# y's step issued in two pieces with other products between them, one convolution moved from TensorE to VectorE, and the loads of later chunks tied to products

## The chip, the cores and the metric

The kernel runs on one core of a Trainium2 chip. The metric is the device time of one execution, in microseconds (us). TensorE is called PE here, its weight loads PEld, VectorE DVE, ScalarE ACT, GpSimd POOL, and the engine that issues the transfers SP. TensorE's clock has two levels, 1.2 and 2.4 GHz; the profile gives the granted clock of a stretch as a share of the higher one.

## The reference

A gated linear attention feeds a gated projection with a short causal convolution. There are 4 batches, 8 heads, 768 steps and a head size of 48; the projection is 384 wide, and the convolution has 5 taps.

```python
# attention, for every batch and head
f = 1.0 / (1.0 + np.exp(-f_logit))
for t in range(S):
    state = f[:, :, t, :, None] * state + np.einsum('bhd,bhe->bhde', k[:, :, t], v[:, :, t])
    y[:, :, t] = np.einsum('bhd,bhde->bhe', q[:, :, t], state)
# projection of x = y with the heads side by side
for k in range(K):
    gate_pre += conv_w[k][None, None, :] * xp[:, k:k + S, :]
gate = 1.0 / (1.0 + np.exp(-gate_pre))
return gate * (x @ w_val) @ w_out
```

## The kernel before

The 768 steps are cut into six chunks (c = 0 to 5) of 128. A tile holds two heads of a pair side by side on the partitions, so four batches of four pairs make 16 blocks of 128 columns. Batches are called b, and h = 0 or 1 is a half, that is two batches.

For a chunk, `loadf`, `loadk`, `loadq` and `loadv` bring the inputs (SP). `pexp`, `pln`, `scan`, `exp2` and `exp1` make the decays (ACT and DVE). `pmulk` and `pmulq` scale k and q by them (DVE). On PE, `ktrans` transposes k, `scores` makes the products of q and k inside the chunk, `dstate` the products of k and v for the state, and `apply` makes y: from the masked scores with v (matmuls that the profile names psum<-asb,vb) and, from chunk 1 on, from q with the state (psum<-qb,st). `mask` (DVE, asb<-psum,tri) puts the scores into SBUF, `kevac` (ACT, ksb<-psum) the transposes, and `xevac` (ACT, xf<-psum) puts y there. `stadd` (DVE, u<-st,psum) and `stmul` (POOL, st<-u,e) carry the state on.

The projection of a chunk follows. `msplit` and `mlow` split y into a high and a low part; `mval` is x @ w_val in nine matmuls; `mout` is the product with w_out, nine more. The convolution has two forms. `pconv` does it on PE, in 120 small matmuls against diagonal matrices (psum<-xf,diag), and `gate` reads its PSUM. `mlast` (ACT) and twelve `mconv` (DVE, gt<-xf,cws,gt) do the same without PE. Chunks 0, 1 and 2 use `pconv`, chunks 3, 4 and 5 `mlast` and `mconv`. The last chunk's projection goes in two halves, numbered 5 and 6. `weight` is one step of the conversion of the 64-bit weights to pairs of float32, spread over POOL, ACT and DVE; `wload` loads them, and `wturn` moves a second copy of w_out within SBUF, for the chunks without `pconv`.

The order of all this work is written out in the string PROGRAM, one word a piece, and every engine does its pieces in exactly that order: the class Ordered ties each instruction of an engine to the one before it. So a piece that has to wait holds up all that stands behind it on its engine. SP's queue, which issues all transfers, is ordered in the same way. PSUM has eight banks, which pieces take and give back in the order of the string.

`apply` for a half h issues two passes, n = 0 and n = 1. Row half r of the array (partitions 0 to 63, or 64 to 127) works on batch 2h + (r ^ n), so that the two row halves never write the same PSUM bank at once. Between the passes stands `PE.drain()`, after which the second pass adds to what the first has written. From chunk 1 on a pass is 96 matmuls, in chunk 0 it is 64. Each matmul is two instructions, a weight load and the product.

Of the kernel before, what the change touches and what calls it, by code (L numbers as in the profile page):

```python
# [37 lines left out]
pmulq 0 0; ktrans 0 3; halo 0; weight 1; kevac 0 0; loadv 0 0; weight 0; scores 0 3; loadv 0 1; weight 0; mask 0 2;
pmulk 0 1; exp1 0 1; pmulq 0 1; weight 1; mask 0 3; ktrans 0 1; pexp 1 0; loadv 0 2; ktrans 0 2; pln 1 0; kevac 0 1;
exp1 1 1; weight 1; scores 0 0; dstate 0 0; scan 1 0; kevac 0 2; mask 0 0; weight 1; weight 0; loadk 1 0; weight 3;  # L40
weight 2; dstate 0 1; exp2 1 0; exp1 1 0; weight 3; scores 0 1; apply 0 1; mask 0 1; dstate 0 2; okc 0; pmulk 1 0;
apply 0 0; weight 2; loadq 1 0; pmulq 1 0; kevac 0 3; loadv 1 0; xevac 0 1; ktrans 1 0; dstate 0 3; kevac 1 0;
weight 2; ktrans 1 1; weight 0; scores 1 1; loadk 1 1; xevac 0 0; weight 2; weight 3; pconv 0; mask 1 1; weight 2;
stadd 0 0; msplit 0; loadf 2 0; weight 2; kevac 1 1; stadd 0 1; pexp 2 0; weight 2; weight 3; scores 1 0; weight 2;
pln 2 0; pmulk 1 1; dstate 1 0; mask 1 0; dstate 1 1; gate 0 2; loadq 1 1; weight 1; weight 3; ktrans 1 2; weight 3;
loadv 1 1; loadf 2 1; apply 1 0; weight 2; loadk 2 0; weight 3; ktrans 1 3; kevac 1 2; wload 2; loadf 3 0; weight 3;
weight 3; loadq 2 1; weight 2; stadd 1 0; pmulq 1 1; weight 5; mlow 0; dstate 1 2; halo 1; scan 2 0; scores 1 2;
gate 0 0; xevac 1 0; scores 1 3; weight 3; gate 0 1; mval 0 0; mval 0 2; mask 1 3; okc 1; weight 4; mask 1 2;
pexp 2 1; pln 2 1; mmul 0 0; loadq 2 0; kevac 1 3; scan 2 1; apply 1 1; exp2 2 0; stmul 1 0; pmulk 2 0; pexp 3 0;
weight 4; weight 4; exp1 2 0; loadv 3 0; loadk 2 1; loadv 2 0; dstate 1 3; mval 0 1; mmul 0 2; weight 5; ktrans 2 1;  # L50
xevac 1 1; pmulq 2 0; exp2 2 1; weight 4; ktrans 2 0; weight 5; scores 2 1; kevac 2 1; stadd 1 1; loadf 3 1; weight 4;
weight 4; kevac 2 0; pmulk 2 1; scores 2 0; mask 2 1; weight 5; exp1 2 1; mhigh 0 2; msplit 1; okc 2; stmul 1 1;
pconv 1; loadq 3 0; weight 4; ktrans 2 2; dstate 2 0; pexp 3 1; weight 4; dstate 2 1; pln 3 1; weight 6; mask 2 0;
kevac 2 2; weight 6; loadf 4 0; mmul 0 1; pln 3 0; apply 2 0; pexp 4 0; loadk 4 0; mlow 1; ktrans 2 3; weight 6;
xevac 2 0; mval 1 2; kevac 2 3; pmulq 2 1; loadv 2 1; stadd 2 0; weight 6; stmul 2 0; mhigh 0 1; scan 3 0; scores 2 3;
mask 2 3; loadq 3 1; weight 5; mval 1 0; loadk 3 0; exp2 3 0; scores 2 2; pln 4 0; loadq 4 0; weight 5; weight 5;
loadf 4 1; weight 6; mhigh 0 0; weight 6; wturn 2; exp1 3 0; mask 2 2; weight 6; mrest 0 0; mrest 0 1; mrest 0 2;
gate 1 0; halo 2; gate 1 2; gate 1 1; scan 3 1; mval 1 1; weight 5; weight 6; apply 2 1; mout 0 0; pmulk 3 0;
ktrans 3 0; exp2 3 1; mmul 1 2; pmulq 3 0; loadf 5 0; dstate 2 2; mout 0 1; dstate 2 3; mstore 0 0; loadk 3 1;
wturn 1; kevac 3 0; ktrans 3 1; xevac 2 1; wturn 0; mout 0 2; pmulk 3 1; loadv 4 0; pexp 4 1; pexp 5 0; mmul 1 0;  # L60
scores 3 0; msplit 2; loadq 4 1; mmul 1 1; kevac 3 1; dstate 3 0; mhigh 1 2; dstate 3 1; mhigh 1 0; stadd 2 1;
pln 4 1; loadv 3 1; scan 4 0; scores 3 1; mask 3 0; loadk 4 1; send 0 0; pln 5 0; stadd 3 0; exp1 3 1; mstore 0 1;
mask 3 1; loadk 5 0; exp2 4 0; mrest 1 0; mstore 0 2; mlow 2; exp1 4 0; scan 4 1; pconv 2; pmulk 4 0; mhigh 1 1;
mrest 1 2; mval 2 2; exp2 4 1; apply 3 0; mrest 1 1; mout 1 0; exp1 4 1; gate 2 1; send 0 1; loadv 4 1; send 0 2;
stmul 2 1; gate 2 0; mstore 1 0; mout 1 1; scan 5 0; pmulq 3 1; loadf 5 1; pmulq 4 0; wturn 3; pmulq 4 1; halo 3;
mval 2 1; xevac 3 0; pmulk 4 1; stmul 3 0; gate 2 2; pexp 5 1; mmul 2 2; scores 3 2; scores 4 1; scores 3 3; exp2 5 0;
mmul 2 1; pln 5 1; mval 2 0; mask 4 1; mout 1 2; mask 3 3; mstore 1 1; ktrans 3 2; send 1 0; scan 5 1; exp1 5 0;
mask 3 2; mmul 2 0; loadq 5 0; pmulk 5 0; mhigh 2 1; mstore 1 2; scores 4 0; mask 4 0; kevac 3 2; mhigh 2 0; send 1 1;
ktrans 3 3; mrest 2 0; apply 3 1; mhigh 2 2; mrest 2 1; scores 4 2; mrest 2 2; kevac 3 3; xevac 3 1; dstate 3 2;
scores 4 3; mlast 3 0; ktrans 4 0; pmulq 5 0; mask 4 2; wturn 4; mconv 3 0 0; mconv 3 0 1; kevac 4 0; dstate 3 3;  # L70
mask 4 3; apply 4 0; mlast 3 1; okc 4; stadd 3 1; mlast 3 2; stmul 3 1; mconv 3 2 0; msplit 3; mconv 3 1 0; mout 2 0;
mout 2 2; exp2 5 1; loadq 5 1; mconv 3 0 2; mconv 3 1 1; apply 4 1; mlow 3; mstore 2 0; dstate 4 0; ktrans 4 1;
loadv 5 0; xevac 4 0; send 2 0; loadk 5 1; mconv 3 2 1; mconv 3 0 3; mstore 2 2; mconv 3 1 2; exp1 5 1; mval 3 1;
scores 5 0; xevac 4 1; halo 4; mconv 3 1 3; kevac 4 1; mout 2 1; okc 5; scores 5 1; dstate 4 1; pmulq 5 1; gate 3 0;
send 1 2; pmulk 5 1; gate 3 1; mmul 3 1; mstore 2 1; mhigh 3 1; mconv 3 2 2; mask 5 1; mconv 3 2 3; wturn 5; halo 5;
ktrans 4 2; gate 3 2; mrest 3 1; mlast 4 1; stadd 4 0; mval 3 2; mval 3 0; ktrans 4 3; mmul 3 2; stmul 4 0; kevac 4 2;
scores 5 2; dstate 4 2; mhigh 3 2; loadv 5 1; mconv 4 1 0; mask 5 0; mconv 4 1 1; kevac 4 3; send 2 2; scores 5 3;
dstate 4 3; mmul 3 0; send 2 1; msplit 4; mrest 3 2; mhigh 3 0; mlow 4; mlast 4 2; mrest 3 0; mconv 4 2 0; apply 5 0;
mask 5 2; mlast 4 0; xevac 5 0; stadd 4 1; mconv 4 2 1; mlast 5 2; mlast 5 0; mconv 4 2 2; mconv 4 1 2; mask 5 3;
mconv 5 0 0; mout 3 0; mout 3 1; mval 4 0; mconv 4 0 0; mstore 3 0; mval 4 2; msplit 5; hint 3; stmul 4 1; okc 3;  # L80
mstore 3 1; mconv 4 0 1; mconv 5 2 0; mconv 4 2 3; mlast 5 1; mconv 5 2 1; apply 5 1; mval 4 1; gate 4 2; mconv 4 1 3;
mout 3 2; mmul 4 2; gate 4 1; mconv 5 0 1; mconv 4 0 2; xevac 5 1; mconv 5 0 2; msplit 6; mconv 5 1 0; mlast 6 2;
mconv 6 2 0; mlow 6; mlast 6 1; mconv 5 0 3; mconv 4 0 3; mlow 5; send 3 0; mval 6 0; mlast 6 0; gate 4 0;
mconv 6 2 1; mhigh 4 2; mval 6 2; mmul 4 1; mhigh 4 1; mval 5 1; mconv 5 2 2; mmul 4 0; mhigh 4 0; mval 5 0; gate 5 0;
mconv 5 1 1; mrest 4 1; mrest 4 2; mconv 5 2 3; mval 6 1; mrest 4 0; mconv 6 2 2; mconv 5 1 2; mconv 5 1 3; mval 5 2;
mconv 6 1 0; mstore 3 2; mconv 6 2 3; gate 5 1; mmul 5 0; gate 5 2; mconv 6 0 0; mhigh 5 0; mmul 5 1; mconv 6 0 1;
mout 4 0; mout 4 1; mmul 5 2; mhigh 5 1; mconv 6 1 1; send 3 1; mconv 6 0 2; gate 6 2; send 3 2; mhigh 5 2;
# [700 lines left out]
```

## Time and profile before

| what | us |
|---|---|
| median of three timed runs | 256.76 (254.6 to 258.27) |
| the profiled execution | 256.75 |
| its span, first to last instruction | 255.0 |
| PE busy, share of the span | 189.5, 74% |
| DVE busy | 163.2, 64% |
| ACT busy | 129.6, 51% |
| POOL busy | 40.9, 16% |
| mean granted clock of PE | 0.928 |

A line of a timeline gives the start, how long the group took, the engine, the operation with the tile that it writes and those that it reads, and the count; what stands in brackets is the idle time of the engine just before it and what ended it. "issue" means that the engine waited for nothing that the profile shows. Nearly all instructions have one line number, that of the helper which orders them, so tiles tell them apart.

### The profile page before, as it was taken

How to read it: one execution, taken by the hardware profiler on the slowest of the kernel's cores; microseconds unless marked ns; L12 is line 12 of the kernel's file. 1: busy time of each engine (PE TensorE's matmuls, PEld its weight loads, DVE VectorE, ACT ScalarE, POOL GpSimd, SP SyncE). 2: the span in 40 equal slices, each digit the busy share in tenths (PEclk: the TensorE clock that was granted, in tenths of full speed). 3: DMA queues.
4: the chain of work that ended last, by engine and by line, in shares of the span. 5: the costliest groups of instructions: out<-in, count | busy, mean ns of one | idle time of the engine just before them, and what ended most of it. 6: DMA issues, size and time to landing. Idle time of an engine off the chain costs nothing. (4 is left out here: it accounts for less than half of the span.)

```text
span 255.0 us, 8960 instructions
## 1 busy us (share of the span) xinstructions
PE 189.5 (74%) x4084; PEld 150.3 (59%) x4084; DVE 163.2 (64%) x228; ACT 129.6 (51%) x203; POOL 40.9 (16%) x47
## 2 busy tenths in 40 slices
...
GB/s 179 394 414 417 389 107 6 226 35 361 112 27 282 17 167 37 312 263 3 136 218 7 124 57 18 157 5 204 109 44 1 5 42 44 3 0 41 59 164 39
DMA packets 11917, 33.30 MB, mean 131 GB/s; under 512 B 1504, under 2 KB 3296, under 8 KB 11616
## 3 DMA queue, kind: packets, MB, share of 16 engines
...
q8 instruction: 34, 0.56, 0.9%
...
## 5 line engine op out<-in xcount | busy, mean ns | idle before, releaser
L106 ACT ACTIVATE e<-e 128x1024 f32<-128x1024 f32 (+2 forms) x58 | 52.4, 930 | 11.2 <-DVE e L106 7.9
L106 DVE TENSOR_TENSOR asb<-psum,tri 128x768 f32<-128x768 f32 x24 | 22.7, 950 | 40.0 <-PE psum L106 28.8
L106 PE MATMUL psum<-asb,vb 64*32 64x64 f32 (+1 forms) x1536 | 29.4, 264 | 16.2 <-issue 15.7
L106 PE MATMUL psum<-rg,woH 128*128 128x512 f32 (+1 forms) x108 | 34.4, 406 | 3.0 <-ACT xf L106 1.9
L106 PEld LDWEIGHTS psum<-asb,vb 64*32 64x32 f32 x1536 | 25.3, 113 | 19.1 <-issue 18.4
L106 ACT COPY xf<-psum 128x768 f32<-128x768 f32 x12 | 9.6, 800 | 42.6 <-PE psum L106 40.0
L106 DVE TENSOR_TENSOR_SCAN e<-keep,e 128x1024 f32<-128x1024 bf16 (+1 forms) x13 | 28.7, 2218 | 4.0 <-ACT e L106 4.0
L106 POOL TENSOR_TENSOR st<-u,e 128x512 f32<-128x512 f32 x8 | 15.4, 1931 | 95.2 <-DVE u L106 81.8
L106 PE MATMUL psum<-ident,kb 128*128 128x128 f32 x80 | 15.5, 331 | 19.2 <-DVE kb L106 16.2
L106 PEld LDWEIGHTS psum<-rg,woH 128*128 128x128 f32 x108 | 20.5, 202 | 7.7 <-ACT xf L106 2.1
L106 PE MATMUL psum<-qb,kb 64*64 64x128 f32 (+1 forms) x768 | 22.2, 259 | 3.4 <-ACT xf L106 2.3
L106 PEld LDWEIGHTS psum<-qb,kb 64*64 64x64 f32 x768 | 19.2, 140 | 8.7 <-ACT xf L106 3.1
L106 PEld LDWEIGHTS psum<-ident,kb 128*128 128x128 f32 x80 | 10.9, 166 | 22.0 <-issue 16.4
L106 ACT COPY osb<-psum 128x512 f32<-128x512 f32 x15 | 8.7, 586 | 26.1 <-PE psum L106 23.5
L106 ACT COPY ksb<-psum 128x384 f32<-128x384 f32 x20 | 9.4, 475 | 23.8 <-PE psum L106 23.8
L106 PE MATMUL psum<-rg,woL 128*128 128x512 f32 (+1 forms) x54 | 21.5, 398 | 0.0
L106 PE MATMUL psum<-xf,diag 32*32 32x512 f32 x360 | 17.4, 652 | 4.7 <-DVE asb L106 4.6
L106 PE MATMUL psum<-xH,wvH 128*128 128x512 f32 x45 | 19.3, 429 | 0.3 <-ACT xf L106 0.3
L106 DVE TENSOR_TENSOR gt<-psum,gt 128x512 f32<-128x512 f32 x15 | 10.1, 685 | 14.5 <-PE psum L106 9.1
L106 DVE SCALAR_TENSOR_TENSOR gt<-xf,cws,gt 128x512 f32<-128x512 f32 x24 | 18.9, 807 | 0.1
L106 PE MATMUL psum<-xL,wvH 128*128 128x512 f32 x45 | 18.2, 405 | 0.0
L106 PE MATMUL psum<-xH,wvL 128*128 128x512 f32 x45 | 18.1, 403 | 0.0
...
## 6 DMA issues: line engine op xcount, KB each, us to landing
e<-in_f SPq DMA_DIRECT2D x11, 512.0 KB, 5.1
kb<-in_k SPq DMA_DIRECT2D x11, 512.0 KB, 5.9
qb<-in_q SPq DMA_DIRECT2D x11, 512.0 KB, 7.2
...
```

The source lines that it names most:

```text
L106: ins = emit(*a, **kw)
```

## The change

- `apply` takes a third number, n, and issues one pass. The drain is gone. A new piece `turn c h` stands in the order between the two passes of a half: a POOL memset of eight numbers (the tile `mark`) that waits for the last PE instruction issued so far, and the first matmul of the second pass waits for that memset. Other PE pieces stand between the passes.
- `load` for chunks 2 and later also waits for the last PE instruction that stands before it in the order.
- The convolution of chunk 2 goes from `pconv` to three `mlast` and twelve `mconv`. So chunk 2's projection uses the second copy of w_out, and the `wturn` pieces come earlier.
- `dstate` makes 48 columns a head and not 64. The state tile st has 80 columns a pair of heads, data in the middle and zeros (one POOL memset at the start) around it; `stadd` and `stmul` handle 48 columns of each.
- The whole order is written anew, under a rule that counts the blocks in which PE's instructions are loaded.

The core of the diff; of the new order, the start, a stretch with chunk 2's convolution, and one line of chunk 5:

```diff
-CONV = "PPPVVV"
+CONV = "PPVVVV"
...
+loadf 0 1; pexp 0 1; pln 0 1; loadf 0 2; loadv 0 1; loadv 0 0; loadf 0 0; loadq 0 1; pexp 0 2; scan 0 1; pln 0 2;
+scan 0 2; loadq 0 0; exp2 0 1; pexp 0 0; loadk 0 2; pln 0 0; loadk 0 0; scan 0 0; loadk 0 1; pmulk 0 1; loadf 1 0;
+wload 0; exp1 0 1; exp2 0 2; pmulq 0 1; loadq 0 2; loadf 2 0; ktrans 0 1; exp2 0 0; pexp 1 0; loadv 0 2; pmulk 0 2;
...
+kevac 0 2; weight 1; pexp 2 0; pmulk 1 0; apply 0 1 0; ktrans 0 3; stadd 0 0; kevac 0 3; apply 0 0 0; weight 2;
+turn 0 0; weight 0; weight 2; weight 1; dstate 0 2; dstate 0 3; loadq 1 0; ktrans 1 1; pmulq 1 0; loadk 1 1; pexp 1 1;
+loadv 1 0; loadv 1 1; ktrans 1 0; kevac 1 0; pln 1 1; turn 0 1; weight 1; kevac 1 1; weight 1; apply 0 0 1; loadq 1 1;
+weight 1; scores 1 0; apply 0 1 1; stadd 0 1; loadk 2 0; weight 1; weight 0; xevac 0 0; xevac 0 1; pln 2 0;
...
+scores 3 3; kevac 3 1; okc 2; mrest 1 2; mrest 1 1; mlast 2 1; loadf 5 0; wturn 5; mconv 2 0 0; wturn 2; mask 3 3;
+apply 3 0 0; turn 3 0; mconv 2 1 0; exp2 4 0; mout 1 0; mask 3 2; dstate 3 0; mlast 2 2; send 0 1; loadq 4 1;
+stmul 2 1; mout 1 1; ktrans 3 2; mconv 2 0 1; exp1 4 0; wturn 4; pexp 5 0; exp2 4 1; mconv 2 1 1; wturn 1;
+mconv 2 2 0; mlow 2; mconv 2 1 2; mconv 2 0 2; dstate 3 1; mconv 2 1 3; kevac 3 2; apply 3 0 1; loadk 4 0; mstore 1 1;
...
+mval 3 2; mask 5 3; apply 5 0 0; mmul 3 2; mhigh 3 2; mrest 3 1; scores 5 2; mrest 3 0; turn 5 0; loadv 5 1; msplit 4;
...
-    st = mp.tile([128, BP, 64], F32, name="st")
+    st = mp.tile([128, BP, 80], F32, name="st")
+    mark = mp.tile([1, 8], F32, name="mark")
-    U = [mp.tile([128, 2 * NP, 64], F32, name=f"u{i}") for i in range(2)]
+    U = [mp.tile([128, 2 * NP, D], F32, name=f"u{i}") for i in range(2)]
...
+    def after(ins, what):
+        tc.add_manual_dep(ins.ins, what.ins.name, mybir.DependencyInfo(mybir.DependencyClass.Sync, mybir.DependencyReason.DATA),
+                          reason="not before that")
     def load(dst, src, c, n):
         x0, x1 = spans["f"](c)[n]
-        SP.dma_start(dst[:, x0:x1], src[c, :, x0:x1])
+        ins = SP.dma_start(dst[:, x0:x1], src[c, :, x0:x1])
+        if c > 1 and PE.last is not None:
+            after(ins, PE.last)
...
+    POOL.memset(st, 0.0)
...
-                us.append((st[rows, x, 32 * (g - r) : 32 * (g - r) + 32], qb[i][rows, x], m, slice(0, C)))
+                us.append((st[rows, x, 16 + 32 * g - 48 * r : 48 + 32 * g - 48 * r], qb[i][rows, x], m, slice(0, C)))
...
-    def apply(c, h):
+    def apply(c, h, n):
+        if n == 0:
+            banks.take(("apply", c, h), 2)
...
-            if n:
-                PE.drain()
...
+            if (c, h) in fence:
+                after(ins, fence.pop((c, h)))
+
+    def turn(c, h):
+        ins = POOL.memset(mark, 0.0)
+        after(ins, PE.last)
+        fence[c, h] = ins
...
-                PE.matmul(dps[s * 64 : s * 64 + 64, n * 64 : n * 64 + 64], KSB[b % 2][:, p, s],
-                          vb[c % NB][:, b * NP + p, 48 * s : 48 * s + 64], start=True, stop=True)
+                PE.matmul(dps[s * 64 : s * 64 + 64, n * D : n * D + D], KSB[b % 2][:, p, s],
+                          vb[c % NB][:, b * NP + p, 64 * s : 64 * s + D], start=True, stop=True)
...
-            DVE.tensor_tensor(out=U[h][:], in0=st[:, HS[h]], in1=dps, op=ALU.add)
+            DVE.tensor_tensor(out=U[h][:], in0=S, in1=dps, op=ALU.add)
```

On PE alone, the new order of the first chunk and a half is: ktrans 0 1; scores 0 1; ktrans 0 0; scores 0 2; scores 0 3; ktrans 0 2; dstate 0 0; dstate 0 1; scores 0 0; apply 0 1 0; ktrans 0 3; apply 0 0 0; dstate 0 2; dstate 0 3; ktrans 1 1; ktrans 1 0; apply 0 0 1; scores 1 0; apply 0 1 1; dstate 1 0; scores 1 1; pconv 0. Its end, from the last half's first pass, is: apply 5 1 0; mval 4 1; mval 4 0; apply 5 1 1; mval 4 2; mout 3 2; mval 5 1; mval 5 2; mval 5 0; mval 6 1; mval 6 2; mval 6 0; and then the mout of 4, 5 and 6. Before, the end was: apply 5 1; mval 4 1; mout 3 2; mval 6 0; mval 6 2; mval 5 1; and on.

## Rows read from the trace of the kernel before

**Rows 1.** The page's first part: busy time of an engine, its share of the span, and its instructions.
```profile
PE 189.5 (74%) x4084; PEld 150.3 (59%) x4084; DVE 163.2 (64%) x228; ACT 129.6 (51%) x203; POOL 40.9 (16%) x47
```
**Rows 2.** Who waited for whom, PE's matmuls alone: us in total, times, the longest in us.
```profile
PE psum L106 <- issue: 18.1, 12, 5.2
PE psum L106 <- DVE kb L106: 16.2, 1, 16.2
PE psum L106 <- DVE asb L106: 12.8, 9, 3.0
PE psum L106 <- ACT xf L106: 4.6, 5, 1.9
```
**Rows 3.** The timeline of PE around stalls that "issue" ended, in both of chunk 0's `apply` and in the first of chunk 1's.
```profile
28.45 1.56 PE L106 MATMUL psum<-asb,vb 64*32 64x64 f32 x83 [0.70 <-issue]
29.94 0.69 PE L106 MATMUL psum<-vb,ksb 128*64 128x64 f32 x16
30.55 0.66 PE L106 MATMUL psum<-asb,vb 64*32 64x128 f32 x28
36.44 2.75 PE L106 MATMUL psum<-asb,vb 64*32 64x128 f32 x100 [5.23 <-issue]
...
52.37 1.00 PE L106 MATMUL psum<-asb,vb 64*32 64x128 f32 x59 [1.43 <-issue]
...
55.70 0.44 PE L106 MATMUL psum<-asb,vb 64*32 64x64 f32 x27 [1.07 <-issue]
```
**Rows 4.** The page's third part, the queue that brings instructions: packets, MB, share of 16 engines.
```profile
q8 instruction: 34, 0.56, 0.9%
```
**Rows 5.** The timeline of PE: one `scores`, the first matmul of an `mval` and the product behind its ninth, two passes of an `apply`, and chunk 2's `pconv` with the product behind it.
```profile
47.59 0.90 PE L106 MATMUL psum<-qb,kb 64*64 64x128 f32 x32
...
95.96 0.51 PE L106 MATMUL psum<-xH,wvH 128*128 128x512 f32 x1
...
98.25 0.90 PE L106 MATMUL psum<-qb,kb 64*64 64x128 f32 x32
...
101.36 0.67 PE L106 MATMUL psum<-qb,st 64*32 64x128 f32 x32
...
102.93 0.67 PE L106 MATMUL psum<-qb,st 64*32 64x128 f32 x32
...
123.90 1.06 PE L106 MATMUL psum<-xf,diag 32*32 32x512 f32 x8 [1.16 <-DVE asb L106]
125.36 4.74 PE L106 MATMUL psum<-xf,diag 32*32 32x512 f32 x112 [0.40 <-DVE asb L106]
130.03 0.50 PE L106 MATMUL psum<-xH,wvH 128*128 128x512 f32 x1
```
**Rows 6.** Busy time by stretch: its length, then PE, PEld, DVE, ACT and POOL busy (instructions), PE's granted clock, the share of the DMA engines, GB/s.
```profile
30.00:45.00 15.00, 9.58 (x266) 7.34 (x277) 4.92 (x9) 4.46 (x7) 0.00 (x0) 0.77 0.25 95
...
105.00:115.00 10.00, 8.68 (x71) 6.70 (x71) 5.83 (x9) 2.86 (x4) 0.00 (x0) 0.66 0.82 290
...
225.00:235.00 10.00, 8.79 (x52) 8.79 (x53) 9.96 (x20) 4.47 (x10) 0.00 (x0) 0.66 0.07 26
```
**Rows 7.** The same view with other stretches: the start, the saturated stretch behind it, the middle, and five us of the middle.
```profile
0.00:16.00 16.00, 0.00 (x0) 0.00 (x0) 10.68 (x12) 11.01 (x17) 5.99 (x20) 1.00 0.87 313
16.00:36.00 20.00, 13.09 (x348) 10.87 (x349) 16.63 (x28) 12.07 (x21) 2.29 (x3) 0.95 0.90 355
...
85.00:165.00 80.00, 65.55 (x1470) 50.42 (x1468) 55.73 (x61) 45.01 (x65) 14.24 (x7) 0.94 0.37 120
...
130.00:135.00 5.00, 4.92 (x191) 4.05 (x188) 5.00 (x6) 4.30 (x5) 0.28 (x1) 1.00 0.44 139
```
**Rows 8.** Groups of instructions with shapes kept apart: count, busy us, mean ns of one, idle before.
```profile
L106 DVE SCALAR_TENSOR_TENSOR gt<-xf,cws,gt 128x512 f32<-128x512 f32 x24 | 18.9, 807 | 0.1
...
L106 DVE TENSOR_TENSOR u<-st,psum 128x512 f32<-128x512 f32 x8 | 5.5, 682 | 8.3 <-ACT xf L106 8.3
...
L106 ACT ACTIVATE gt<-xf,cws 128x512 f32<-128x512 f32 x6 | 4.2, 722 | 1.6 <-DVE rg L106 1.5
...
L106 POOL MEMSET ones<- 128x1 f32 x1 | 0.1, 93 | 0.0
```
**Rows 9.** The start, in the timelines of DVE (two rows) and of PE (one).
```profile
8.73 5.87 DVE L106 TENSOR_TENSOR_SCAN e<-keep,e 128x1024 f32<-128x1024 bf16 x3 [2.50 <-ACT e L106]
14.53 1.93 DVE L106 TENSOR_TENSOR kb<-kb,e 128x512 f32<-128x512 f32 x4
...
16.23 1.19 PE L106 MATMUL psum<-ident,kb 128*128 128x128 f32 x4 [16.23 <-DVE kb L106]
```
**Rows 10.** The timeline of PE's weight loads at the second pass of an `apply`, and that of POOL at the longest of its products.
```profile
67.58 0.41 PEld L106 LDWEIGHTS psum<-qb,st 64*32 64x32 f32 x32 [0.24 <-issue]
...
134.72 5.16 POOL L106 TENSOR_TENSOR st<-u,e 128x512 f32<-128x512 f32 x1 [13.43 <-PE psum L106]
```
**Rows 11.** Transfers by line: count, KB each, median us from issue to landing.
```profile
kb<-in_k SPq DMA_DIRECT2D x11, 512.0 KB, 5.9
qb<-in_q SPq DMA_DIRECT2D x11, 512.0 KB, 7.2
```
**Rows 12.** The timeline of PE where the last half's y has to reach the projection.
```profile
224.41 0.39 PE L106 MATMUL psum<-re,wvH 128*128 128x256 f32 x1 [1.75 <-ACT re L106]
226.21 0.58 PE L106 MATMUL psum<-re,wvH 128*128 128x256 f32 x1 [1.41 <-DVE re L106]
```

More of the change, by code (lines that the diff above doesn't have):

```diff
@@ L38 @@
[L38 to L87, printed above, removed]
@@ new lines @@
+scan 0 2; loadq 0 0; exp2 0 1; pexp 0 0; loadk 0 2; pln 0 0; loadk 0 0; scan 0 0; loadk 0 1; pmulk 0 1; loadf 1 0;
+wload 0; exp1 0 1; exp2 0 2; pmulq 0 1; loadq 0 2; loadf 2 0; ktrans 0 1; exp2 0 0; pexp 1 0; loadv 0 2; pmulk 0 2;
+exp1 0 2; pmulk 0 0; scores 0 1; pmulq 0 2; ktrans 0 0; halo 0; pln 1 0; scan 1 0; scores 0 2; loadk 1 0; weight 0;
+weight 0; kevac 0 0; exp1 0 0; weight 0; pmulq 0 0; weight 0; scores 0 3; wload 1; ktrans 0 2; kevac 0 1; mask 0 2;
+weight 1; dstate 0 0; dstate 0 1; exp2 1 0; exp1 1 0; loadf 1 1; mask 0 3; weight 0; mask 0 1; scores 0 0; mask 0 0;
@@ new lines @@
+weight 2; exp1 1 1; mask 1 0; pconv 0; mask 1 1; weight 3; weight 3; pmulk 1 1; pmulq 1 1; weight 3; apply 1 0 0;
+ktrans 1 3; gate 0 2; turn 1 0; weight 2; dstate 1 1; weight 3; weight 3; weight 3; scores 1 3; gate 0 0; weight 2;
+okc 1; ktrans 1 2; apply 1 0 1; wload 2; weight 4; okc 0; loadf 3 1; kevac 1 3; weight 3; weight 3; stadd 1 0; mlow 0;
+loadv 2 0; scores 1 2; gate 0 1; mval 0 0; weight 4; mask 1 3; weight 2; pexp 2 1; weight 3; mask 1 2; weight 5;
+kevac 1 2; weight 4; apply 1 1 0; weight 3; stmul 1 0; weight 1; weight 1; turn 1 1; loadv 2 1; loadq 2 0; dstate 1 2;
@@ new lines @@
+weight 4; weight 5; mval 0 2; dstate 1 3; pln 2 1; scan 2 0; weight 4; weight 4; loadf 4 0; exp2 2 0; scan 2 1;
+weight 4; halo 1; exp1 2 0; pmulk 2 0; weight 4; apply 1 1 1; loadv 3 0; loadq 2 1; mval 0 1; pexp 3 1; xevac 1 0;
+stadd 1 1; xevac 1 1; weight 6; weight 6; msplit 1; mmul 0 0; mmul 0 2; weight 6; ktrans 2 0; weight 5; mmul 0 1;
+ktrans 2 1; wturn 0; pexp 4 0; loadf 3 0; exp2 2 1; weight 5; kevac 2 0; stmul 1 1; loadf 4 1; kevac 2 1; loadk 2 1;
+exp1 2 1; mhigh 0 2; pln 3 1; weight 6; mhigh 0 1; weight 5; weight 6; pmulq 2 0; loadq 3 0; mlow 1; weight 6;
@@ new lines @@
+pconv 1; scores 2 1; weight 6; mhigh 0 0; mask 2 1; pexp 3 0; loadk 3 0; weight 6; pln 3 0; loadq 3 1; scores 2 0;
+dstate 2 0; weight 5; pmulk 2 1; pexp 4 1; mask 2 0; halo 2; dstate 2 1; weight 5; mrest 0 0; weight 5; pln 4 1;
+mval 1 2; ktrans 2 2; stadd 2 0; apply 2 0 0; mrest 0 2; gate 1 0; mrest 0 1; kevac 2 2; mval 1 0; loadv 3 1;
+scan 3 0; scan 3 1; loadk 3 1; turn 2 0; mmul 1 0; apply 2 0 1; mval 1 1; pmulq 2 1; dstate 2 2; gate 1 2; gate 1 1;
+pln 4 0; xevac 2 0; mout 0 1; exp2 3 0; scan 4 1; scores 2 3; scores 2 2; mstore 0 1; pmulk 3 0; mmul 1 2; mask 2 3;
@@ new lines @@
+mask 2 2; exp2 3 1; mmul 1 1; exp1 3 0; loadv 4 0; loadq 4 0; pmulq 3 0; mout 0 0; scan 4 0; ktrans 2 3; ktrans 3 0;
+apply 2 1 0; mout 0 2; pmulk 3 1; ktrans 3 1; mstore 0 0; send 0 0; kevac 2 3; exp1 3 1; turn 2 1; stmul 2 0;
+scores 3 0; mhigh 1 0; mstore 0 2; apply 2 1 1; kevac 3 0; scores 3 1; mrest 1 0; mask 3 0; pmulq 3 1; send 0 2;
+mhigh 1 1; dstate 2 3; xevac 2 1; mhigh 1 2; mask 3 1; ktrans 3 3; msplit 2; stadd 2 1; mlast 2 0; scores 3 2;
+scores 3 3; kevac 3 1; okc 2; mrest 1 2; mrest 1 1; mlast 2 1; loadf 5 0; wturn 5; mconv 2 0 0; wturn 2; mask 3 3;
@@ new lines @@
+gate 2 2; pln 5 0; xevac 3 0; stmul 3 0; pexp 5 1; mmul 2 2; apply 3 1 1; mout 1 2; scores 4 1; okc 3; pln 5 1;
+pmulq 4 1; wturn 3; pmulk 4 1; mmul 2 0; mhigh 2 2; mval 2 1; scan 5 0; mstore 1 2; xevac 3 1; mhigh 2 0; mask 4 1;
+mrest 2 2; mmul 2 1; scores 4 0; scores 4 2; halo 3; scores 4 3; loadk 5 0; loadq 5 1; dstate 3 3; mask 4 0; mask 4 2;
+exp2 5 0; ktrans 4 0; mhigh 2 1; mrest 2 0; msplit 3; ktrans 4 1; kevac 4 0; ktrans 4 2; apply 4 0 0; stadd 3 1;
+mrest 2 1; dstate 4 0; loadk 5 1; kevac 4 1; mlast 3 1; turn 4 0; scan 5 1; mlast 3 0; send 1 2; mlow 3; mconv 3 0 0;
@@ new lines @@
+loadq 5 0; dstate 4 1; exp1 5 0; kevac 4 2; mconv 3 0 1; mask 4 3; mout 2 1; exp2 5 1; mconv 3 0 2; apply 4 0 1;
+mconv 3 0 3; mconv 3 1 0; mout 2 0; stmul 3 1; ktrans 4 3; mlast 3 2; mconv 3 1 1; kevac 4 3; pmulk 5 0; exp1 5 1;
+send 1 1; pmulk 5 1; mstore 2 1; apply 4 1 0; loadv 5 0; mval 3 1; gate 3 0; send 2 1; mstore 2 0; mconv 3 1 2;
+dstate 4 2; mconv 3 1 3; dstate 4 3; mconv 3 2 0; mconv 3 2 1; pmulq 5 0; xevac 4 0; stadd 4 0; turn 4 1; pmulq 5 1;
+apply 4 1 1; send 2 0; xevac 4 1; stmul 4 0; halo 4; mconv 3 2 2; mout 2 2; gate 3 1; mmul 3 1; mstore 2 2; mval 3 0;
```

63 lines of the change are left out of this document (36 added, 27 removed).

## The prediction

> **What bounds the kernel now.** I read the page's first part to see which engine is fullest, then PE's waits to see where the rest of its time is, then its timeline at the largest waits, and the busy time by stretch for its clock and for what the others have to spare. PE is the fullest, with 189.5 us of the span's 255.0; DVE has 163.2 [rows 1]. The first matmul starts at 16.2 us [rows 9], and after PE's last, at 247.6, some 7.4 us of stores and closing work follow. Between these PE has about 231.4 us, so some 42 us of it are idle. "Issue" ends 18.1 us of that, DVE's masks 12.8 and ACT's copies of y 4.6 [rows 2], and the wait for the last half's y 3.2 [rows 12]. The reader is to see that the largest of these is no data at all.
>
> The "issue" stalls stand inside `apply`, and at even distances: from the one at 28.45 us to the one at 36.44 there are 83 + 16 + 28 = 127 matmuls [rows 3], with their weight loads 254 instructions. The instruction queue moved 0.56 MB in 34 packets, 16.5 KB each [rows 4]. Were a packet 254 instructions, one would be 65 bytes, and PE's 2 x 4084 [rows 1] would make 0.53 MB, nearly all that the queue moved. So PE stops where it has run through a block before the next has come. From 28.45 to 36.44 the next one took 8.0 us, with the DMA engines 90% busy [rows 3, 7]; from 52.37 to 55.70 it took 3.3 [rows 3]. An `apply` of both passes is 192 matmuls, and one pass takes 102.93 - 101.36 = 1.57 us [rows 5], so a block of 127 inside it lasts 2.1 us. That is too short to hide 3.3.
>
> There is a second loss. After idle time PE runs at the lower clock level for part of a stretch: the mean is 0.77 from 30 to 45 us and 0.66 from 105 to 115 (both behind long "issue" stalls), and 0.66 from 225 to 235 [rows 6]. Busy time times the missing share gives 9.58 x 0.23 = 2.2, 8.68 x 0.34 = 3.0 and 8.79 x 0.34 = 3.0 us, worked out from these rows.
>
> **The change part by part.** The sum starts at the profiled execution's 256.75 us, 0.01 below the median of 256.76, so nothing is lost between them.
>
> *Blocks and the two pieces.* I counted the matmuls of both orders in steps of 127 and added up PE's work in each step, a piece at the time from its start to that of the next, such as 1.57 us for a pass or 98.25 - 95.96 = 2.3 for an `mval` [rows 5]. Before, 11 blocks hold less than 2.5 us of work; after, 4 do, since an `mval` or `mout` stands between most passes. The four are at chunk 0's second passes, before chunk 3's first, where apply 3 0 1 and 3 1 0 are adjacent, and around chunk 5's scores 5 2. The two stalls of chunk 0 made 5.9 us [rows 3]; the other ten share 12.2, some 1.2 each. After: 4 x 1.2 = 4.9, and 2.5 more for the start, where the DMA engines stay saturated [rows 7] but chunk 0's blocks get 3.7 and 4.3 us of work. That is 7.4 instead of 18.1, -10.7; the bounds are 0 and -18.1.
>
> The Trainium skill ("Runtime: NRT & Kernel Launch", section "Instruction fetch mechanics") says that instructions come in 16 KiB blocks of 256, the next fetched while the current one runs, and that the cost of a block's end is mostly hidden. The trace agrees on the block, with 254 instructions and 16.5 KB, and not on the hiding, with 18.1 us. By that rule this term would be nothing and the sum 10.7 higher; that is a rival below.
>
> *The drain.* It goes from twelve places. The second pass's weight load stands 0.24 us behind the first pass's [rows 10]; part of that any switch of tiles would cost. I take -2 in all, bounds 0 and -2.9.
>
> *The token.* The memset has a neighbour of 93 ns [rows 8]. With the two hand-overs it is a few tenths. The shortest cover is one `scores`, 0.90 us [rows 5], so I cost it at nothing where POOL is free. If POOL is not, the second pass waits: behind `turn 1 1` stand five weight steps and `stmul 1 0`, and one product on POOL took 5.16 us [rows 10]. I take +1; bounds 0 and +5.
>
> *The convolution of chunk 2.* PE loses the `pconv` from 123.90 to 130.03, 5.7 us without its waits of 1.6 [rows 5]: -5.7. DVE gains 12 x 0.79 = 9.5 us (18.9 / 24) and ACT 3 x 0.72 = 2.2 [rows 8]. DVE has 80 - 55.7 = 24.3 us to spare from 85 to 165, but none in stretches such as 130 to 135 [rows 7]. What hides the twelve is that spare time; where it is gone, masks and `pmulk` come late and PE waits as it did for 12.8 us. The bounds are 0 and +11.7; I take about half, +5.5.
>
> *Narrower state.* A `stadd` of 512 columns takes 682 ns [rows 8]; a quarter less of each of eight gives DVE 1.4 us at most, an estimate; `dstate` issues as many matmuls as before. The memset of st at the start runs while POOL has 10 us to spare [rows 7]. I take -0.5, bounds 0 and -2.
>
> *The start.* Before, DVE did three scans (5.87 us from 8.73) and two `pmulk` before the first `ktrans` [rows 9]; one scan was chunk 1's. The new order leaves that one out and asks for one `pmulk`, of quarter 1. With two scans, about 3.6 us, and 0.8 for the product it comes to 13.2. The loads ahead of it are 3.0 MB; at the start's mean 313 GB/s [rows 7] that is 9.6 us, before which it is hidden, and I add half a microsecond. -2.5, bounds 0 and -3.
>
> *The clock.* With the long stalls gone I take half of the first two stretches' 5.2 us: -2.6, bounds 0 and -5.2.
>
> *The end.* Behind the last pass stood an `mval` and a `mout` before the first product that needs the last half's y; now there are three half-width `mval` more, each half of a 2.3 us product. They cover the 3.2 us of [rows 12]; I take -2.7, and nothing for the clock there. Bounds 0 and -6.
>
> *The later loads.* Each now waits for a product that the order puts well before its use; the shortest distance I find is `loadk 2 1`, issued behind ktrans 2 1 and used after pconv 1 and the pass of scores behind it, some 6 us on, against 5.9 to landing [rows 11]. SP's queue behind a waiting load holds other loads, `wturn` and stores. I take 0, bounds -2 and +26 (below).
>
> Sum: -10.7 - 2 + 1 - 5.7 + 5.5 - 0.5 - 2.5 - 2.6 - 2.7 = -20.2, which is 236.5; I say 236.
>
> **The rivals.** *DVE becomes the bound.* All of the 9.5 and the 2.2 us end up in PE's waits: 6.2 more, and the token's bound with it: about 244. For it: the full stretches [rows 7]. Against it: the spare 24.3 us.
>
> *Instructions come late all the same.* The stalls keep their 18.1 us, at other places, since fetches are slow under loads: 236.5 + 10.7, about 247. For it: the 8.0 us fetch [rows 3]. Against it: 3.3 us where DMA was calmer, and the loads are now spread. The skill's rule named above leads to the same number, for another reason, that the stalls never were fetches.
>
> *Both of these*, 236.5 + 10.7 + 6.2 = 253.4, no change.
>
> *Loads late behind products: slower.* In each of chunks 2 to 5 PE waits for one load of q or k of 5.9 to 7.2 us [rows 11] that was issued as it was needed: 4 x 6.55 = 26.2 gives 263. It decides from about 20 us on, three such waits. For it: one queue in strict order, and most of these loads were issued early before. Against it: the distances above.
>
> *The waits shrink too.* If the 12.8 us for masks [rows 2] fall by 8, as more work stands between a mask and its pass, and the twelve `mconv` find spare time, it is 225.
>
> **How the numbers follow.** The forecast has 0.44, DVE as the bound 0.17, late instructions 0.15, both 0.10, late loads 0.07, shrinking waits 0.07. The forecast's own range is 230 to 242. The range of 226 to 250 takes in the first three and part of the last, and leaves out about 0.2. A change of less than 2%, 5.1 us, can't be told from none here: faster is under 251.6, slower over 261.9. The first three and the last make 0.83, less some spill of the upper ones: 0.80. No change has the case of both and that spill, less what of late loads is slower: 0.13. Slower: 0.07.
>
> **What the profile of the changed kernel would show.** If the blocks are right, "issue" ends 5 to 9 us of PE's waits and hardly any stands at a second pass. If the start is right, the first matmul is at 13 to 14 us. PE's busy time should be near 180, and DVE's near 171. If the token is late, PE waits for POOL's `mark`, first at apply 1 1 1. If DVE binds, the waits for masks grow beyond 15 us between 90 and 130 us. If loads are late, PE or DVE wait for kb or qb behind a DMA. The forecast is wrong above all if the "issue" row stays over 14 us, or if the masks take what it gives back.

## The result

The changed kernel takes 223.79 us (median of 4 runs, 222.83 to 225.06) against 255.68 for the kernel before in the same job. The ratio is 0.8833, 95% interval 0.8723 to 0.8943: about 12% faster. That is 12 us under the forecast of 236 us and 2.2 under the low end of its range, 226 to 250. A ratio here and below compares only the faster runs of a kernel, those within 1.5% of its fastest, so it is not the quotient of the medians. The profiled execution took 224.42 us, 32.3 less than before's.

The page's first part for the kernel after, in answer to [rows 1]:

```profile
span 222.6 us, 8753 instructions
PE 177.0 (80%) x3964; PEld 143.3 (64%) x3964; DVE 168.7 (76%) x240; ACT 130.3 (59%) x206; POOL 32.7 (15%) x60
```

Who PE's matmuls waited for in the kernel after, in answer to [rows 2] (us in total, times, the longest):

```profile
PE psum L110 <- DVE asb L110: 16.7, 12, 5.3
PE psum L110 <- DVE kb L110: 13.3, 2, 13.1
PE psum L110 <- issue: 6.5, 5, 2.2
PE psum L110 <- DVE qb L110: 0.9, 2, 0.4
PE psum L110 <- POOL mark L110: 0.8, 3, 0.3
PE psum L110 <- POOL st L110: 0.5, 1, 0.5
PE psum L110 <- ACT xf L110: 0.5, 2, 0.2
```

With the busy times these make an account of the span as PE sees it:

| PE's time, us | before | after | difference |
|---|---|---|---|
| ahead of the first matmul | 16.2 | 13.1 | -3.1 |
| busy | 189.5 | 177.0 | -12.5 |
| "issue" | 18.1 | 6.5 | -11.6 |
| masks (asb) | 12.8 | 16.7 | +3.9 |
| y into SBUF (xf) | 4.6 | 0.5 | -4.1 |
| the last half's y (re) | 3.2 | none | -3.2 |
| others of those shown | 2.3 | 2.2 | -0.1 |
| behind the last matmul | 7.4 | 6.5 | -0.9 |

The reader is to see three things. The waits on instructions fell as the prediction had it. PE's busy time fell by twice the work that was taken from it. And the waits for masks grew by about as much as those for y into SBUF fell, a row for which the prediction's sum has no term.

The timeline of PE in the kernel after, around what is left of "issue", in answer to [rows 3]:

```profile
13.07 1.19 PE L110 MATMUL psum<-ident,kb 128*128 128x128 f32 x4 [13.07 <-DVE kb L110]
...
24.36 0.35 PE L110 MATMUL psum<-asb,vb 64*32 64x64 f32 x16 [0.64 <-issue]
...
30.29 1.02 PE L110 MATMUL psum<-asb,vb 64*32 64x128 f32 x60 [1.59 <-issue]
...
33.85 0.45 PE L110 MATMUL psum<-asb,vb 64*32 64x64 f32 x29 [1.06 <-issue]
...
44.17 0.74 PE L110 MATMUL psum<-asb,vb 64*32 64x128 f32 x38 [2.22 <-issue]
...
122.11 1.02 PE L110 MATMUL psum<-asb,vb 64*32 64x128 f32 x61 [0.99 <-issue]
```

From 50 us on a single one is left, where the passes 3 0 1 and 3 1 0 are adjacent; the other four lie in chunk 0 and at the first pass of chunk 1. The last of these four, at 44.17, stands behind 127 matmuls with 4.5 us of work, more than half of a `pconv` among them; while they ran, the DMA engines were busy for 0.77 of the time. The first row answers to [rows 9]: PE starts at 13.07.

PE's groups with shapes kept apart (count, busy us, mean ns) show where busy time went:

```profile
L110 PE MATMUL psum<-xf,diag 32*32 32x512 f32 x240 | 9.9, 592 | 0.5 <-POOL st L110 0.5
L110 PE MATMUL psum<-re,wvH 128*128 128x256 f32 x36 | 6.2, 276 | 0.0
L110 PE MATMUL psum<-re,wvL 128*128 128x256 f32 x18 | 5.0, 276 | 0.0
```

Before, the same view has 17.4 us at 652 ns for `pconv` and 9.2 and 6.2 us, at 353 and 346 ns, for the last half's `mval`. Of the 7.5 us less for `pconv`, 5.7 are chunk 2's. Most of the rest is chunk 1's, in the timelines of before and after:

```profile
77.90 6.63 PE L106 MATMUL psum<-xf,diag 32*32 32x512 f32 x120 [3.02 <-DVE asb L106]
```

```profile
65.54 4.93 PE L110 MATMUL psum<-xf,diag 32*32 32x512 f32 x120 [0.46 <-POOL st L110]
```

The last half's two groups overlap in time, so their busy times can't be added. By the timelines, that `mval` took 9.3 us before (from 224.41 to 235.13, less a wait of 1.41) and takes 6.1 after (196.94 to 203.08). That is 3.2 us less, and the granted clock went with it: 0.66 from 225 to 235 in [rows 6], and 1.00 at this end in after:

```profile
192.00:205.00 13.00, 13.00 (x140) 11.71 (x127) 12.01 (x25) 8.28 (x17) 0.00 (x0) 1.00 0.06 21
```

### The profile page after: what moved, and what is told of

Same layout as the page of the kernel before. It is cut to its first block, busy times and chain, and to the rows that moved or that the text cites. A ratio compares the mean times of both kernels' runs of the same rounds, so it can differ in the third digit from the quotient of the medians.

```text
span 222.6 us, 8753 instructions
## 1 busy us (share of the span) xinstructions
PE 177.0 (80%) x3964; PEld 143.3 (64%) x3964; DVE 168.7 (76%) x240; ACT 130.3 (59%) x206; POOL 32.7 (15%) x60
## 4 chain that ended last, share of the span: by engine, by line
PE 61%; DVE 21%; DMA 5%; issue 5%; ACT 3%; SPq 0%; POOL 0%; DVEq 0%; ACTq 0%
PE psum L110 61%; DVE asb L110 5%; DVE gt L110 5%; DMA e<-in_f 3%; DVE xL L110 3%; DMA vb<-in_v 2%; DVE e L110 2%; DVE qb L110 2%; ACT xf L110 1%; DVE rg L110 1%; DVE cb L110 1%; ACT e L110 1%; DVE kb L110 1%; DVE ca L110 1%; DVE u L110 1%
## 5 line engine op out<-in xcount | busy, mean ns | idle before, releaser
L110 DVE TENSOR_TENSOR asb<-psum,tri 128x768 f32<-128x768 f32 x24 | 22.5, 953 | 19.6 <-PE psum L110 13.7
L110 PE MATMUL psum<-asb,vb 64*32 64x128 f32 (+1 forms) x1536 | 27.1, 251 | 6.7 <-issue 6.5
L110 PEld LDWEIGHTS psum<-asb,vb 64*32 64x32 f32 x1536 | 24.1, 107 | 8.7 <-issue 7.8
L110 DVE TENSOR_TENSOR_SCAN e<-keep,e 128x1024 f32<-128x1024 bf16 (+1 forms) x13 | 27.4, 2116 | 3.0 <-ACT e L110 3.0
L110 PE MATMUL psum<-qb,kb 64*64 64x128 f32 (+1 forms) x768 | 24.4, 278 | 4.9 <-DVE asb L110 4.1
L110 PEld LDWEIGHTS psum<-qb,kb 64*64 64x64 f32 x768 | 21.5, 155 | 9.5 <-DVE asb L110 5.2
L110 DVE SCALAR_TENSOR_TENSOR gt<-xf,cws,gt 128x512 f32<-128x512 f32 x36 | 25.8, 745 | 0.2
L110 PE MATMUL psum<-ident,kb 128*128 128x128 f32 x80 | 13.8, 309 | 13.8 <-DVE kb L110 13.3
L110 DVE TENSOR_TENSOR kb<-kb,e 128x512 f32<-128x512 f32 (+1 forms) x26 | 16.6, 685 | 4.4 <-DMA kb<-in_k 2.4
L110 POOL MEMSET mark<- 1x8 f32 x12 | 1.1, 95 | 121.8 <-PE psum L110 121.8
L110 PE MATMUL psum<-qb,st 64*32 64x128 f32 x640 | 14.7, 282 | 4.6 <-DVE asb L110 3.3
```

The lines of the kernel that those rows point to most:

```text
L110: ins = emit(*a, **kw)
```

## The experiments

Times are medians, against the kernel after at 223.8 us (224.2 in its second job) or before at 255.0 to 257.6, by job. The jobs ran on different chips, so a difference of 1 or 2 us between jobs can't be told from none.

**The old order with the new parts.** Token for drain, the narrower state, no waits in the loads:

```diff
-apply 0 1;
+apply 0 1 0; turn 0 1; apply 0 1 1;
```

> The order of before, with the drain replaced by the POOL token (the two passes still adjacent, so PE waits for the token each time), the 48-column state, and no wait in the loads; chunk 2 keeps its pconv. Theory (the gain is in the order: blocks of instructions, the packing of work, the clock): within 3 us of before either way, issue still ends 16 to 20 us of PE's waits, and POOL's mark adds some 0.3 us at each of twelve places. Rival (the drain itself and the wide state cost much): 6 us or more below before.

It took 257.4 us (253.4 to 259.8), before 256.1 beside it. Its waits of PE:

```profile
PE psum L112 <- issue: 14.8, 9, 4.1
...
PE psum L112 <- POOL mark L112: 3.2, 12, 0.3
```

"Issue" ends 14.8 us, a little under the 16 to 20 that I expected. Without products between the passes the token is paid at every pass, 3.2 us for twelve. The parts alone are worth nothing that can be told; the gain needs the order.

**Shifting the blocks.** 64 one-column matmuls ahead of all else, in the kernel before:

```diff
+    for _ in range(64):
+        PE.matmul(P[0:32, 0, 0:1], idle[:, 0:32], idle[:, 0:1], start=True, stop=True)
     run(PROGRAM, pieces)
```

> The kernel before with 64 one-column matmuls ahead of all others, in PE's idle start. Theory (a stall stands where PE comes to the end of a block of 127 matmuls): every issue stall moves by 63 or 64 matmuls of the order; in chunk 0 from the 45th matmul of the first apply to about the 108th, and from the 28th of the second to about the 91st. Rival (the stall belongs to the passes, the drain or a semaphore): they stay where they were.

PE's timeline of this kernel in chunk 0's two `apply`:

```profile
27.36 1.92 PE L106 MATMUL psum<-asb,vb 64*32 64x128 f32 x108
31.07 0.62 PE L106 MATMUL psum<-asb,vb 64*32 64x64 f32 x20 [1.79 <-issue]
31.62 1.13 PE L106 MATMUL psum<-vb,ksb 128*64 128x64 f32 x16
32.68 2.40 PE L106 MATMUL psum<-asb,vb 64*32 64x128 f32 x92
35.87 0.73 PE L106 MATMUL psum<-asb,vb 64*32 64x128 f32 x36 [0.79 <-issue]
```

The stalls stand behind matmul 108 of the first and 92 of the second: they follow the count, not the pass and not the drain. And with nothing else changed "issue" fell from 18.1 to 9.1 us. The one run took 247.8, against 251.7 to 261.0 for seven of before in this job and 249.8 for the fastest of before in any job; what the shift is worth in time lies between 2 and 10 us. My count of blocks with less than 2.5 us of work falls from 10 to 5 by this shift. The trace of before has the same grid by itself: eleven of its twelve stalls, all but one of 0.16 us, lie on it, and from the first at 28.45 to the last at 217.98 there are 3695 matmuls, 29 steps of 127.4.

**The passes together again,** in the order of after, with the drain:

```diff
-apply 1 1 0; weight 3; ...; turn 1 1; ...; dstate 1 3; ...; apply 1 1 1;
+apply 1 1 0; apply 1 1 1; weight 3; ...; dstate 1 3;
```

> The order of after, but the second pass of each apply directly behind the first, with the drain between them and no token. Nine blocks of 127 matmuls then hold less than 2.5 us of work instead of four. Theory (stalls come where a block is too short): issue goes from 6.5 to 12 to 16 us, and the time up by 6 to 12 us. Rival (the gain is the rest of the order): within 3 us of after.

It took 237.5 us (236.3 to 241.0), 13.7 above after, somewhat more than the 6 to 12 of the theory; ratio to before 0.929 (0.9246 to 0.9334). Its waits, and two of its stalls in the timeline:

```profile
PE psum L112 <- issue: 15.6, 12, 3.2
PE psum L112 <- DVE asb L112: 14.2, 12, 2.4
```

```profile
155.93 0.86 PE L112 MATMUL psum<-asb,vb 64*32 64x128 f32 x50 [1.29 <-issue]
...
189.47 0.34 PE L112 MATMUL psum<-asb,vb 64*32 64x64 f32 x15 [1.15 <-issue]
```

"Issue" is up by 9.1 us and PE's busy time by 3.4 (180.4) at the same number of matmuls; from 45 to 55 us the granted clock was 0.65. The two make 12.5 of the 13.7.

**The drain with the passes apart.**

```diff
-turn 1 1; 
+            if n:
+                PE.drain()
```

> The kernel after with the drain in place of the token; the passes stay apart. It shows what the token alone is worth, where other products stand between. My sum had 2 us for the drain and 1 for a late token. Theory: within 2 us of after. Rival (a drain holds the products behind it back by more): 3 us or more above after.

226.7 us (226.1 to 228.6), some 2.7 above after. The one theory allowed up to 2 and the other asked for 3 or more, so the run decides neither; taken as measured, across two jobs, the token is worth some 2.7 us here, and the passes apart the other 11 of the 13.7.

**The passes apart in the old order.** The second pass goes behind the next one or two PE pieces:

```diff
-apply 1 1; exp2 2 0; ...; dstate 1 3; mval 0 1;
+apply 1 1 0; turn 1 1; exp2 2 0; ...; dstate 1 3; mval 0 1; ...; apply 1 1 1;
```

> The order of before with one thing moved: the second pass of each apply goes behind the next one or two PE pieces (apply 5 0 has none and stays as it was), with the token. Blocks with less than 2.5 us of work fall from 10 to 3. The rest is as in the first run with the old order. Theory (short blocks are what stalls PE): issue from 14.8 to 6 to 9 us, time 5 to 10 us below before. Rival (the gain of the passes apart needs the rest of the new order): less than 3 us below.

250.6 us, 7 below before, within what the theory asked; but the four runs go from 242.8 to 252.4, so the size is uncertain (fastest against fastest, in this job, it is 8.9). "Issue" was 12.2 in its profile, more than the 6 to 9 that I expected: 5.8 of it are the two stalls of chunk 0, where loads are the cause as well.

**Chunk 2's convolution left out of DVE,** that is, four of its five taps are not computed at all; and in a second job the same beside after on one chip:

```diff
-mconv 2 0 0; ...; mconv 2 1 0; ...; mconv 2 2 3;
```

> The kernel after without the twelve mconv of chunk 2 on DVE: this leaves out four of the five taps of chunk 2's convolution. It shows what they cost. My prediction had 5.5 us of them on the path. Theory (they fit into DVE's idle time): 0 to 3 us faster than after. Rival (DVE is the bound there): 5 to 9 us faster.

> The kernel after, for the two runs beside it on one chip: 222 to 226 us.

> The kernel after without the twelve mconv of chunk 2 (four taps of its convolution are left out). If they fit into DVE's idle time: 0 to 2 us below the kernel after beside it. If half of them is on the path, as my sum had it: 4 to 6 us below.

222.8 us in the first job; in the second 222.9 (220.3 to 225.7), with after at 224.2 (223.1 to 224.8) beside it. PE's waits in that run:

```profile
PE psum L112 <- DVE asb L112: 17.4, 13, 5.3
...
PE psum L112 <- issue: 7.5, 4, 3.9
```

DVE had 8 us less to do (160.5), and PE waited for masks as long as ever (17.4; after beside it 17.9). The twelve cost some 1.3 us, which lies within the spread of the runs.

**Chunk 2's convolution back on PE:**

```diff
-mlast 2 0; ...; mconv 2 0 0; ...; gate 2 1; ...; gate 2 0; ...; gate 2 2;
+pconv 2; gate 2 1; gate 2 0; gate 2 2;
```

> The order of after with chunk 2's convolution on PE again, behind the scores of chunk 3, and its three gates right behind it. Theory (DVE had room for the twelve, as the run without them showed, so PE's 5.7 us are gained in full): 5 to 9 us slower than after, PE's busy time up by 5 to 6. Rival (the move was a trade, with DVE giving back what PE gains): within 2 us of after.

231.2 us (229.2 to 232.7), 7.4 above after; ratio 0.9112 (0.8952 to 0.9273).

```profile
PE 182.5 (80%) x4084; PEld 146.0 (64%) x4084; DVE 160.6 (70%) x228; ACT 128.6 (56%) x203; POOL 32.6 (14%) x60
```

```profile
PE psum L112 <- DVE asb L112: 17.2, 12, 5.3
```

PE's busy time is 5.5 us up, and the masks come no sooner for DVE's 8 us less. The move was no trade. Of the other 1.9 us the waits for masks make 0.5; the rest is within what two jobs can differ by.

**Both undone:** the passes together with the drain, and `pconv 2` on PE.

> The order of after with two parts undone at once: the passes together with the drain, and chunk 2's pconv on PE. Alone they cost 13.7 and 7.4 us. Theory (they add, and what is left below before is the rest of the order): 241 to 248 us, so some 8 to 15 us of the gain are neither of the two. Rival (they overlap, or the whole gain lies in these two): under 238, or over 252.

243.0 us (236.0 to 244.9), where 224 + 13.7 + 7.4 = 245 would be exact addition. Three of the four runs are at 241 to 245; the fourth, at 236.0, is where the rival had it, so the addition holds by the median and not by each run. The other 12 us below before belong to the rest of the change, its order above all, since the new parts in the old order brought nothing. The profile shows where they lie:

```profile
PE psum L111 <- issue: 15.5, 11, 2.9
PE psum L111 <- DVE asb L111: 14.9, 14, 2.1
...
PE psum L111 <- ACT xf L111: 1.5, 1, 1.5
```

Against before, PE starts 3.0 us earlier (13.2), is busy 5.1 us less (184.4) at the same number of matmuls, waits 2.6 less on "issue", 3.1 less for y into SBUF and not at all for the last half's y (3.2), and 2.1 more for masks. That is 14.9 of the 15.6 us between the two profiled executions.

**The loads of w_val early:**

```diff
-loadk 1 0; weight 0; ...; wload 1;
+loadf 0 0; wload 1;
```

> The kernel after with one load moved: the 1152 KB of w_val go right behind loadf 0 0, ahead of chunk 0's k and q, about where before had them. k then lands some 2.9 us later (1152 KB at about 400 GB/s). Theory (the earlier start of PE reaches the end, as the sum had it with 2.5 us): first matmul at 15 to 16.5 us instead of 13.1, time 2 to 4 us above after. Rival (DVE, not PE, sets the first 60 us, and the weights come earlier): within 1 us of after.

224.9 us (224.4 to 226.4), 1.1 above after, between the theory's 2 to 4 and none. PE started 3 us later, and at `pconv 0` only 1.1 us were left of that:

```profile
16.05 1.19 PE L114 MATMUL psum<-ident,kb 128*128 128x128 f32 x4 [16.05 <-DVE kb L114]
...
36.77 5.09 PE L114 MATMUL psum<-xf,diag 32*32 32x512 f32 x120
```

In after the same `pconv` starts at 35.66. Two thirds of the late start are absorbed.

**The loads without their waits,** twice:

```diff
-        if c > 1 and PE.last is not None:
-            after(ins, PE.last)
```

> The kernel after, its loads without the wait for a product, so they start as soon as their buffers are free. Theory (the waits of the loads matter little, the blocks have 4 us of work where loads run): within 2 us of after. Rival (the waits keep loads away from fetches of instructions): issue grows from 6.5 to 10 us or more and the time by 3 us or more. Second rival (loads come late in after): 2 us or more faster.

> The kernel after without the waits of the later loads. If the waits keep loads away from fetches of instructions: 2 to 4 us above the kernel after beside it. If they matter little: within 1.5 us.

226.9 us (224.9 to 233.1), and 229.5 (225.0 to 230.6) beside after's 224.2, more than the 2 to 4 that I expected of waits that matter. "Issue" was 7.3 us in the profile of a run of 224.9, and 9.7 in one of 229.1; both have stalls of 2.9 us at chunk 3's adjacent passes, where after has 0.99. The 127 matmuls ahead of that stall, in the kernel after and in the first of these runs (the columns of [rows 6]):

```profile
119.10:122.11 3.01, 2.02 (x133) 1.75 (x131) 3.01 (x5) 2.99 (x5) 0.00 (x0) 1.00 0.44 139
```

```profile
117.58:122.53 4.95, 2.02 (x133) 1.75 (x131) 4.92 (x8) 4.72 (x7) 0.00 (x0) 1.00 0.98 370
```

PE had the same 2.02 us of work in both. With the DMA engines busy for 0.98 of the time and not 0.44, the block took 1.9 us longer. In time, three of the ten runs lie at 224.9 to 225.2, some 1 us above after, and seven from 228.7 to 233.1; what parts the two groups is not settled. So 1 us of the waits' worth can be told, up to 5 by the second job's median, and they cost nothing.

**One mask earlier.** The longest wait of after is 5.3 us for a mask. `mout 2 1`, which had it, reads no mask, and DVE did a scan, `mlow 3` and two `mconv` ahead of that mask:

```profile
146.93 0.95 DVE L110 TENSOR_TENSOR asb<-psum,tri 128x768 f32<-128x768 f32 x1
```

The edit puts it ahead of them:

```diff
-mask 4 0; mask 4 2; ... mconv 3 0 1; mask 4 3;
+mask 4 0; mask 4 2; mask 4 3; ... mconv 3 0 1;
```

> The kernel after with one piece moved: mask 4 3 right behind mask 4 2 on DVE, ahead of a scan, the low part of chunk 3 and two mconv. In after PE stood 5.28 us before mout 2 1 until that mask was done, and then ran 4 us at the lower clock. Theory (mout 2 1 waits for a PSUM bank that the scores of mask 4 3 hold): that wait goes, 4 to 8 us faster than after. Rival (other work of DVE holds PE there): within 2 us of after.

217.2 us (213.8 to 221.6), some 6.8 below after; the ratio of 0.851 has a wide interval, 0.8199 to 0.8821. PE's timeline at that `mout`, in after and then with the mask early:

```profile
141.51 1.14 PE L110 MATMUL psum<-vb,ksb 128*64 128x48 f32 x32
147.93 1.22 PE L110 MATMUL psum<-rg,woH 128*128 128x512 f32 x2 [5.28 <-DVE asb L110]
```

```profile
139.40 1.14 PE L114 MATMUL psum<-vb,ksb 128*64 128x48 f32 x32
140.47 0.74 PE L114 MATMUL psum<-rg,woH 128*128 128x512 f32 x2
```

The busy time by stretch, from 140 to 155 us, in both (the columns of [rows 6]):

```profile
140.00:155.00 15.00, 9.72 (x238) 7.91 (x237) 14.86 (x19) 4.46 (x7) 1.30 (x2) 0.77 0.43 148
```

```profile
140.00:155.00 15.00, 13.58 (x371) 10.83 (x366) 14.79 (x19) 8.61 (x13) 1.41 (x4) 1.00 0.54 175
```

The wait went, and with it the stretch at the lower clock level behind it: 1.22 us for two matmuls against 0.74.

The tie is not the one that I expected, a bank that the scores hold. Followed through the order of after, `mout 2 1` gets bank 5, which `stadd 3 1` had given back, and the scores of `mask 4 3` hold banks 3 and 7. The mask reads these two as one strided view of the tile `psum`; the product into a bank between them waited for it, as if the view covered all from 3 to 7. The copies of y in before fit this: eight of the twelve start just as a later product ends that went into a bank between the two of their pair. No run tests this tie by itself.

**That, and the blocks shifted by 20.** By the count this leaves one short block of four.

```diff
+    for _ in range(20):
+        PE.matmul(P[0:32, 0, 0:1], idle[:, 0:32], idle[:, 0:1], start=True, stop=True)
```

> The kernel with mask 4 3 early, and 20 one-column matmuls ahead of all others. By the count of blocks, this leaves one block with less than 2.5 us of work instead of four. Theory: issue from 6.6 to 3 to 5 us, time 1 to 4 us below the run with mask 4 3 early (217.2). Rival (what issue is left comes from loads at the start): no change.

216.5 us (214.8 to 220.3), ratio 0.8544 (0.8476 to 0.8612), which lies wholly below that of after. "Issue" was 4.3 us, as the theory had it. The time is 0.8 below the run without the shift, from another chip, where the theory asked for 1 to 4: the same. So the mask is the version that beats both kernels, and the shift adds nothing that can be told.

## Why the prediction was wrong, step by step

The direction and the main mechanism held; the size was off by 12 us, and more than half of that is one term, the convolution's.

*Blocks.* Right in the mechanism. The term was -10.7, and "issue" fell by 11.6. The shift by 64 shows the cause by itself, and the passes together give back 13.7 us with the drain. Of the four stalls that I expected at short blocks, two came, at chunk 0's second passes and between 3 0 1 and 3 1 0; the other three of after are at the start, under loads. That the size came out is partly luck: the two have 2.1 us where I had 4.9 for four, and the three at the start have 4.5 where I had allowed 2.5, behind blocks of more than 4 us of work. So less than 2.5 us of work was not the whole condition. By the Trainium skill ("Runtime: NRT & Kernel Launch", section "Instruction fetch mechanics") a block's end is mostly hidden. The traces agree with its block of 256 instructions, with some 255 from stall to stall, and show up to 18.1 us that were not hidden. The rival that went with the rule, the stalls staying at 18.1, is out. The reading of the 8.0 us was off: 90% is the mean from 16 to 36 us [rows 7], and from 28.45 to 36.44 the DMA engines were busy for 0.64 of the time.

*The convolution of chunk 2.* This is the step that failed: "-5.7" for PE and "+5.5" for DVE and ACT, because half of their work was to land in PE's waits. The move gave 7.4 us in full. The twelve cost 1.3, and without them the waits for masks were the same. I read spare time from a stretch of 80 us and full five-microsecond pieces from inside it, and split the difference. The waits for masks were the thing to look at. They did grow, by 3.9 us, but the run with chunk 2's `pconv` back on PE has them too, 17.2 us, so they belong to the new order and not to the twelve; from 90 to 130 us, where the twelve stand, they make 4.7 us. The largest of them comes from the place of one mask in DVE's order, as the early mask shows; the others were not tried.

*The clock.* -2.6 was too little. Busy time fell by 12.5, of which chunk 2's `pconv` is 5.7. Of the other 6.8, 1.7 are chunk 1's `pconv` and 3.2 the last half's `mval`, each at a higher granted clock; for the second I had taken nothing.

*The drain and the token.* -2 and +1 stood against some -2.7. PE waited 0.8 us for `mark` in all, three times; no late token came at apply 1 1 1, so that rival price was empty.

*The start.* -2.5 at the first matmul was right, 3.1; at the end of the kernel it is worth about 1.1, by one pair of runs from two jobs.

*The end.* The term of -2.7 was right, 3.2 us of waits for the last half's y, and too narrow. From the last pass to the end of the span it was 255.0 - 218.3 = 36.7 us, and it is 222.6 - 192.7 = 29.9. Another 3.2 are the clock above. In before, the last copy of y stood until `mout 3 2` had ended, at 222.67; in after it starts as the pass ends:

```profile
217.98 0.34 PE L106 MATMUL psum<-asb,vb 64*32 64x64 f32 x13 [1.11 <-issue]
...
222.70 0.80 ACT L106 COPY xf<-psum 128x768 f32<-128x768 f32 x1 [10.76 <-PE psum L106]
```

```profile
191.68 1.02 PE L110 MATMUL psum<-asb,vb 64*32 64x128 f32 x64
...
192.74 0.80 ACT L110 COPY xf<-psum 128x768 f32<-128x768 f32 x1 [7.42 <-PE psum L110]
```

*No term.* PE's waits for y into SBUF fell from 4.6 to 0.5 us. The prediction named them and put them at nothing, without a reason.

*The later loads.* 0 was a little low, by 1 us that can be told. The rival that they come late is out: without their waits the kernel is not faster.

*Two sums.* DVE as the bound is 236.5 + 6.2 = 242.7, and 246.7 with the token's bound of +5 for its +1, not 244; and the shrinking waits, 8 and 5.5 us less, make 223, not 225.

Put together by the experiments: -20.2, another 7.2 for the convolution, 1.7 for the token, 1 for the loads, and 1.4 less for the start, is -28.7, against 31.9 by the medians and 32.3 by the profiled executions. It comes this close partly by luck. Blocks, clock, drain and token, with the last two at what they measured, are -16.0, and undoing them gave back 13.7; the rest, narrower state, start, end and loads, is -5.3, and the run with both undone lies 12 below before. So the convolution is some 7 of the 12 us that the forecast missed, and most of the others lie in what it put at nothing: the clock at the end and the waits for y into SBUF. The nearest rival was "the waits shrink too", 225, to which I gave 0.07. Half of it was so: the twelve found spare time, but the waits for masks did not shrink, they grew by 3.9. Which single move in the new order brought which part of this was not tried.
